# Group 0 of chunks 3 to 6 multiplied by blocks too, with one maximum instruction per head and the lower words behind the scaling

## The chip, the cores and the metric

The kernel runs on one core of a Trainium2 chip, in one launch. The time is device microseconds of the whole program. A core has a matrix engine (TensorE, PE in the profile, whose weight loads are listed as PEld), a vector engine (VectorE, DVE), a scalar engine (ScalarE, ACT), a general engine (GpSimd, POOL) and a queue that issues most DMAs (SyncE, SP). Each engine takes its instructions in the order in which the program lists them.

## The reference

All data is float32 (the inputs arrive as 64-bit floats and are scaled and split on the chip). Eight batches of eight heads attend over 576 positions of 64 values; scores that lie more than tau under the largest of their row are dropped. The heads are put side by side into rows of 512, and these 4608 rows go through a gated feed-forward block:

```python
scores = scale * np.matmul(q, k.transpose(0, 1, 3, 2))
thresh = np.max(scores, axis=-1, keepdims=True) - tau
scores = np.where(scores >= thresh, scores, -1000000000.0)
scores = scores - np.max(scores, axis=-1, keepdims=True)
attn = np.exp(scores)
attn = attn / (np.sum(attn, axis=-1, keepdims=True) + 1e-09)
x = np.matmul(attn, v)                 # (8, 8, 576, 64), then rows (4608, 512)
g = x @ w_gate                         # (512, 1536)
val = x @ w_val
out = (g / (1.0 + np.exp(-g))) * val @ w_out
```

## The kernel before

**Stages.** The work of the eight batches is interleaved. While the attention of batch b is computed, the feed-forward block of batch b - 1 ("chunk" c = b - 1) runs between its pieces. In the head (0 to about 126 us) the first batch's attention runs alone with a start of the feed-forward products, and the weights are split and joined from their 64-bit words: ScalarE takes the upper words (line 360) and the lower words (361), GpSimd clamps and adds (353, 397), VectorE shifts and joins (380, 387). From 126 to 1126 us come the main slots, 84 of them, and from there to 1334 us a tail with the products of the last batches.

**Main slots.** A pair of heads is done in three slots, so a chunk has twelve, kk = 0 to 11, of some 12 us each. A slot starts with the scores of two heads (`slot_scores`, 32 matmuls of 64x32 weights, line 2108) into two score tiles of two PSUM banks each (`ps_s`, a pool of two). Each head has three tiles u = 0, 1, 2 of 288 scores a partition. `slot_rest` then gives out jobs: VectorE finds the maximum of each tile (2129, 2131), the maxima of two partition groups are exchanged and joined (`largest` on VectorE, lines 2137 and 2138, or `others` on ScalarE, 2143, with 2147 on VectorE; the table MAX_BY_ACT says in which slots ScalarE does it), ScalarE computes a threshold (2150) and six exponentials (2154), VectorE six masks with their sums (2156), ScalarE exchanges the sums (2165), VectorE adds and inverts them (2171, 2172), ScalarE and GpSimd scale (2184, 2181; the table POOLED says how many tiles GpSimd takes), and VectorE transposes (2186). The next slot's scores write the same two tiles and wait for all six masks. In each slot with kk = 1, 4, 7, 10 the attention product of the pair before (`attend`, 2208) stands ahead of the scores.

**Gate and value products.** `gates_and_values(c)` goes through six groups g of 256 hidden columns. Each group takes seven products p1 to p7 instead of eight (a block scheme of Strassen's kind over two token halves and two halves of the model dimension), each of four matmuls of 128x128 weights with 256 moving columns, into three PSUM banks named pa, pb and pe. The banks come from four that are handed round (`take`). A copy of pa into pb by ScalarE starts the second accumulation. p5 and p3 go into pe, and ScalarE copies between them.

**Nested groups.** In chunks from DEEP = 2 on, some groups apply the scheme once more inside p5 and p3 (`NestedGroup`): seven matmuls of 128x128 weights and 128 moving columns into two banks in place of four of 256 columns. The inputs are quarters of the token sums that `deepen_x` makes on VectorE in slot kk = 1, from sums that GpSimd makes after the attention product of the same slot (`token_sums`). ScalarE copies both banks out (`Seven.fill`, 1320 and 1322), and four additions fold the seven results into a square (`Seven.fold`), on VectorE or GpSimd as the table FOLDS says. WITH_BLOCKS names the nested groups: 1, 2, 3 (in chunk 2 only 2 and 3). After a group's gate comes a hyperbolic tangent on ScalarE (1245), a multiplication on VectorE (1246) that frees the bank, and one on GpSimd.

**Output products.** `Deep` multiplies by the output weights in eight steps, in slots 9, 10, 11 and in slots 0 and 1 of the next chunk. Its last step, p3, stands in slot 1 between the scores and group 0's p1; its two banks are copied out by ScalarE (1839, 1840).

**Order.** Steps are generators. The table GV says how many steps of products follow the scores in slot kk: 3, 6, 4 in slots 1, 2, 3. Jobs of the other engines are ordered by a planner (`Plan`) when the program is built: each has a fixed planned length, dependences and a rank (0 first). The planner holds a clock per engine and puts the job next that could start first, rank before readiness; before each product it puts in the jobs that start by then. So the order of VectorE, ScalarE, GpSimd and the DMA queue is fixed when the program is built, and the chip adds only waits. Helpers record for many places: 968 is every GpSimd addition (`pool_tt`), 975 every VectorE one (`dve_tt`), 1187 every flat product (`Group.mul`), 1382 every nested one.

Of the kernel before, what the change touches and what calls it, by code (L numbers as in the profile page):

```python
# [157 lines left out]
def kernel(  # L158
# [12 lines left out]
    P = 128  # L171
# [27 lines left out]
    qkp = ctx.enter_context(tc.tile_pool(name="qkp", bufs=2))  # L199
    stp = ctx.enter_context(tc.tile_pool(name="stp", bufs=4))  # L200
    ps_s = ctx.enter_context(tc.tile_pool(name="ps_s", bufs=2, space=bass.MemoryType.PSUM))
    hbm = ctx.enter_context(tc.tile_pool(name="hbm", bufs=1, space=bass.MemoryType.DRAM))
# [151 lines left out]

    def split_weights():
        if fetched:
            dst, place = fetched.popleft()
            lo = los[0].rearrange("p (m n) -> p m n", m=dst.shape[1])
            los.rotate(1)
            nc.scalar.activation(dst, words(place, dst, 1).bitcast(F32), AF.Abs, scale=2.0 ** -96)  # L360
            nc.scalar.activation(lo, words(place, dst, 0), AF.Identity, bias=minus2, scale=-2.0 ** -51)
            unclamped.append(dst)
            if early_slots[0]:
                clamp_split()
            split.append((dst, place, lo))

    def clamp_split():
# [117 lines left out]
    def statistics(*names):  # L485
        return [stp.tile([P, 2 * NU3, 2] if x == "mx" else [P, 2 * NU3], F32, name=x) for x in names]

# [324 lines left out]
    for n, seg in enumerate(segs[:2 * NP]):  # L812
# [3 lines left out]
        for x, t in enumerate(seg["tiles"]):  # L816
# [39 lines left out]
            if n >= NP:  # L856
                split_weights()
                fetch_weights(2)
            steps(n, x, "flipped")
            next(go)  # L860
            steps(n, x, "masked")
            double = t == NT and NP <= n < NP + 3
# [447 lines left out]
    class Seven(Buf):  # L1310
# [6 lines left out]
        def fill(self, banks_, m, rank):  # L1317
            t, old = self.place, self.jobs
            self.jobs = []
            return [job("ACT", 0.46, lambda: nc.scalar.activation(t[:, 4 * P:CW], banks_[1].ap()[:, 0:3 * P], AF.Copy, scale=0.5),  # L1320
                        m, *old, rank=rank),
                    job("ACT", 0.57, lambda: nc.scalar.activation(t[:, 0:4 * P], banks_[0].ap(), AF.Copy, scale=0.5), m, *old, rank=rank)]  # L1322

# [28 lines left out]
    def deepen_x(c, *deps):  # L1352

        ts = *(x_main[:, n * 2 * P:(n + 1) * 2 * P] for n in range(3)), tmp.rearrange("p a f n -> p (a f n)")[:, 4 * HW:4 * HW + 2 * P]
        deps = *deps, *s_bufs[0].jobs
        t1, t2, t4, t3 = (x.rearrange("p (o q) -> p o q", o=2) for x in ts)
        x = xall[:, 3 * XW:3 * XW + 3 * HW].rearrange("p (o k n) -> p o k n", o=3, k=2)[:, 0:3:2]
        b11, b12, b21, b22 = (x[:, :, k_, n * P:(n + 1) * P] for k_ in range(2) for n in range(2))
        deps = *ready_x[c][1], *ready_x[c][4], *deps
        rank = 1  # L1360
        j = job("DVE", 0.36, dve_tt(t1, b12, b11, ALU.subtract), *deps, rank=rank)
        j = job("DVE", 0.36, dve_tt(t2, b22, t1, ALU.subtract), j, rank=rank)
        j = job("DVE", 0.36, dve_tt(t4, b21, t2, ALU.subtract), j, rank=rank)
# [728 lines left out]
    def slot_scores(seg, t):  # L2092
# [20 lines left out]
    def slot_rest(seg, t, pss, mark, pooled, max_by_act, rank):  # L2113
# [7 lines left out]
        at_of = lambda h, u: seg["p"] + (2 * (NU3 * t + u) + h) * SH  # L2121
        scs = {(h, u): pss[h][:, u, 0:SH] if u < 2 else pss[h][:, :, SH:SH + SQ] for h, u in tiles}
        flat = {x: pall[:, at_of(*x):at_of(*x) + SH] for x in tiles}
        ps = {x: y if x[1] < 2 else y.rearrange("p (a n) -> p a n", a=2) for x, y in flat.items()}
        n_of = lambda h, u: NU3 * h + u
        rs = []
        for h, tile_ in enumerate(pss):
            n = n_of(h, 0)
            rs.append(job("DVE", 0.72, lambda n=n, tile_=tile_: nc.vector.tensor_reduce(  # L2129
                out=mx[:, n:n + 2, 0], in_=tile_[:, :, 0:SH], axis=AX.X, op=ALU.max, negate=True), mark, rank=0))  # L2130
            rs.append(job("DVE", 0.42, lambda n=n, tile_=tile_: nc.vector.tensor_reduce(  # L2131
                out=mx[:, n + 2:n + 3, 0], in_=tile_[:, :, SH:SH + SQ], axis=AX.XY, op=ALU.max, negate=True), mark, rank=0))

        def largest():
            for g in range(NG):
                o = g ^ 1
                nc.vector.tensor_reduce(out=mx[g * G:(g + 1) * G, 0:m, 1], in_=mx[o * G:(o + 1) * G, 0:m, 0:1], axis=AX.X, op=ALU.max)
            nc.vector.tensor_reduce(out=nm[:, 0:m], in_=mx[:, 0:m, :], axis=AX.X, op=ALU.min)

        def others():  # L2140
            for g in range(NG):
                o = g ^ 1
                nc.scalar.copy(mx[g * G:(g + 1) * G, 0:m, 1], mx[o * G:(o + 1) * G, 0:m, 0])

        if max_by_act:
            oj = job("ACT", 0.78, others, *rs, rank=0)
            nj = job("DVE", 0.18, lambda: nc.vector.tensor_reduce(out=nm[:, 0:m], in_=mx[:, 0:m, :], axis=AX.X, op=ALU.min), oj, rank=0)
        else:
            nj = job("DVE", 0.82, largest, *rs, rank=0)
# [127 lines left out]
    def gates_and_values(c):  # L2277
# [490 lines left out]
```

## Time and profile before

| | us |
|---|---|
| median of 3 runs | 1332.65 (1332.35 to 1334.19) |
| profiled execution | 1336.15 |
| its span | 1334.4 |
| TensorE busy | 1323.6 (99%) |
| its weight loads busy | 1121.6 (84%) |
| VectorE busy | 1092.5 (82%) |
| GpSimd busy | 944.4 (71%) |
| ScalarE busy | 898.3 (67%) |
| scores start in slot 3 of chunks 3, 4, 5, 6 | 575.42, 719.40, 863.37, 1007.58 |

The profile is of one execution; a median is of several. The granted clock of TensorE is 1.00 over the whole span. A line of the timeline has the start in us from the span's start, the length, engine, line, operation, output and inputs, shapes and count; in brackets is the idle time before it and what ended it. Each float32 matmul leaves two records of TensorE, so a flat product shows as x8 and a nested one as 14 records in several lines. A list of waits has the waiting engine, tile and line, then what it waited for, the total, how many times, and the longest.

### The profile page before, as it was taken

The numbers are of one execution on the slowest core, as the hardware profiler recorded it, in microseconds if no ns is written. First come the engines' busy times: TensorE is split into PE (matmuls) and PEld (weight loads), VectorE is DVE, ScalarE is ACT, GpSimd is POOL, SyncE is SP. The second block draws the span as 40 slices with busy tenths as digits, with TensorE's granted clock in tenths as the row PEclk, the third lists the DMA queues.
The fourth block names the chain that finished last, engine by engine and source line by source line (L and its number), as shares of the span: only waits on it lengthen the run. The fifth ranks groups of instructions, "written<-read, shape, count | busy, mean of one in ns | idle before, by whom it ended". The sixth has DMA issues, their size and how long they took to land.

```text
span 1334.4 us, 41739 instructions
## 1 busy us (share of the span) xinstructions
PE 1323.6 (99%) x16294; PEld 1121.6 (84%) x16294; DVE 1092.5 (82%) x2900; ACT 898.3 (67%) x2343; POOL 944.4 (71%) x1130
## 2 busy tenths in 40 slices
PE   9999999999999999999999999999999999999998
PEld 7777777777888888888888888888888889999998
DVE  7889888888887787888888887888788888767987
ACT  6898876676756777787777777777778774444300
POOL 2688587565695969857895779677985798866720
PEclk9999999999999999999999999999999999999999
DMA  8863324456647653656365736655375627465341
GB/s 175 211 191 99 79 61 132 128 147 178 173 152 227 168 167 102 197 165 221 75 201 171 234 101 186 190 158 162 106 214 146 218 74 226 148 210 187 97 171 40
DMA packets 230884, 209.81 MB, mean 157 GB/s; under 512 B 167968, under 2 KB 185376, under 8 KB 223008
## 3 DMA queue, kind: packets, MB, share of 16 engines
q1 hardware_dynamic: 226768, 206.22, 52.5%
q8 instruction: 129, 2.11, 0.7%
q10 hardware_dynamic: 3920, 0.92, 0.3%
q14 instruction: 67, 0.55, 0.1%
HBM read 169.08 MB, written 38.01 MB: 155 GB/s over the span
## 4 chain that ended last, share of the span: by engine, by line
PE 93%; ACT 3%; DMA 1%; POOL 1%; DVE 1%; SPq 1%; issue 0%; ACTq 0%; DVEq 0%
PE pb L1187 14%; PE px L1817 12%; PE sc L2108 10%; PE pa L1187 10%; PE xa L2208 9%; PE pe L1187 6%; PE po L1495 6%; PE sc L2598 5%; PE py L1817 4%; PE pe L1382 3%; PE pb L2598 2%; PE pa L2598 2%; PE pg L1420 2%; PE pv L1420 2%; PE py L1826 2%; PE sc L502 1%
## 5 line engine op out<-in xcount | busy, mean ns | idle before, releaser
L2156 DVE SCALAR_TENSOR_TENSOR pall<-sc,th,pall 128x288 f32<-128x288 f32 x504 | 244.2, 514 | 39.5 <-ACT pall L2154 20.1
L2154 ACT ACTIVATE pall<-sc,nm 128x288 f32<-128x288 f32 x504 | 232.7, 497 | 35.3 <-DVE pall L2156 35.1
L1187 PE MATMUL pb<-xall,big 128*128 128x256 f32 x864 | 205.9, 381 | 0.0
L2186 DVE STREAM_TRANSPOSE pall<-pall 128x576 f32<-128x576 f32 x252 | 188.4, 764 | 19.2 <-ACT pall L2184 9.4
L968 POOL TENSOR_TENSOR big<-big 128x128 f32<-128x128 f32 (+3 forms) x226 | 167.2, 748 | 43.5 <-ACT big L1322 21.7
L2184 ACT ACTIVATE pall<-pall,ri 128x288 f32<-128x288 f32 x380 | 175.8, 527 | 28.2 <-DVE ri L2172 27.1
L1187 PEld LDWEIGHTS pb<-xall,big 128*128 128x128 f32 x864 | 161.0, 190 | 24.1 <-issue 2.2
L968 POOL TENSOR_TENSOR hall<-hall,tmp 128x512 f32<-128x512 f32 x80 | 102.1, 1278 | 88.0 <-DVE hall L1246 65.0
L2129 DVE TENSOR_REDUCE mx<-sc 128x2 f32<-128x576 f32 x168 | 125.6, 747 | 45.7 <-PE sc L2108 45.6
L2108 PE MATMUL sc<-kT,qT 64*32 64x288 f32 (+1 forms) x5376 | 144.5, 345 | 0.8 <-DVE pall L2156 0.8
L1187 PE MATMUL pa<-xall,big 128*128 128x256 f32 x576 | 137.6, 382 | 0.0
L2108 PEld LDWEIGHTS sc<-kT,qT 64*32 64x32 f32 x5376 | 95.2, 106 | 49.1 <-issue 8.3
L2208 PE MATMUL xa<-pall,vall 64*32 64x288 f32 x4032 | 128.7, 404 | 0.0
L1187 PEld LDWEIGHTS pa<-xall,big 128*128 128x128 f32 x576 | 107.9, 190 | 17.3 <-issue 2.2
L2208 PEld LDWEIGHTS xa<-pall,vall 64*32 64x32 f32 x4032 | 73.9, 107 | 47.0 <-issue 4.0
L2181 POOL TENSOR_SCALAR pall<-pall,ri 128x288 f32<-128x288 f32 x124 | 63.5, 524 | 49.7 <-DVE ri L2172 47.7
L2165 ACT COPY sums<-sums 32x6 f32<-32x6 f32 x336 | 66.6, 198 | 31.4 <-DVE pall L2156 26.3
L1187 PE MATMUL pe<-xall,big 128*128 128x256 f32 x352 | 83.9, 381 | 0.0
L2131 DVE TENSOR_REDUCE mx<-sc 128x1 f32<-128x288 f32 x168 | 75.0, 446 | 0.0
L1187 PEld LDWEIGHTS pe<-xall,big 128*128 128x128 f32 x352 | 66.3, 190 | 10.3 <-ACT xlast L2220 0.7
L968 POOL TENSOR_TENSOR hall<-hall 128x384 f32<-128x384 f32 (+2 forms) x69 | 70.5, 1034 | 0.8
L968 POOL TENSOR_TENSOR big<-hall 128x384 f32<-128x384 f32 (+2 forms) x69 | 65.7, 973 | 4.2 <-PE pa L1187 4.1
(400 smaller groups left out, 3065.4 us busy)
## 6 DMA issues: line engine op xcount, KB each, us to landing
big<-sums_hbm SPq DMA_DIRECT2D x30, 1280.0 KB, 7.5
big<-sums_hbm SPq DMA_DIRECT2D x30, 1024.0 KB, 8.1
vall<-in_v_dram SPq DMA_DIRECT2D x112, 144.0 KB, 4.1
big<-sums_hbm SPq DMA_DIRECT2D x54, 256.0 KB, 3.5
sums_hbm<-big SPq DMA_DIRECT2D x36, 256.0 KB, 3.6
out_dram<-big SPq DMA_DIRECT2D x32, 256.0 KB, 2.9
qT<-in_q_dram SPq DMA_DIRECT2D x112, 72.0 KB, 4.2
kT<-in_k_dram SPq DMA_DIRECT2D x112, 72.0 KB, 2.9
```

The lines of the kernel that those rows point to most:

```text
L968: nc.gpsimd.tensor_tensor(out=out, in0=a, in1=b, op=op)
L1187: nc.tensor.matmul(ps[:, i], w[:, k_, i * P:(i + 1) * P], x[:, k_, :], start=first and i == k_ == 0, stop=True, skip_group_check=True)
L1495: nc.tensor.matmul(ps, h(f), w[:, f, :], start=(f == 0), stop=(f == NF2 - 1))
L1817: nc.tensor.matmul(ps, a[:, f, :], ws[n][:, f, :], start=bank_ not in begun, stop=True, skip_group_check=True)
L2108: nc.tensor.matmul(pss[h][(slice(g * G, (g + 1) * G), *part)], qT[hs, col:col + G], kT[hs, c * SH + keys[0]:c * SH + keys[1]], start=True, ...
L2129: rs.append(job("DVE", 0.72, lambda n=n, tile_=tile_: nc.vector.tensor_reduce(out=mx[:, n:n + 2, 0], in_=tile_[:, :, 0:SH], axis=AX.X, op= ...
L2154: ej = job("ACT", 0.42, lambda x=x, n=n: nc.scalar.activation(ps[x], scs[x], AF.Exp, bias=nm[:, n:n + 1]), ej, masks.get((h, u - 1)), rank=0)
L2156: masks[x] = job("DVE", 0.45, lambda x=x, n=n: nc.vector.scalar_tensor_tensor(out=ps[x], in0=scs[x], scalar=th[:, n:n + 1], in1=ps[x], op0 ...
L2184: scaled.append(job("ACT", 0.46, lambda x=x, n=n: nc.scalar.activation(x, x, AF.Copy, scale=ri[:, n:n + 1]), rj, rank=rank))
L2186: seg["turned"].append(job("DVE", 0.72, lambda both=both: nc.vector.transpose(out=both, in_=both), *scaled, rank=rank))
L2208: nc.tensor.matmul(holds[a].ap()[x * G:(x + 1) * G, 0:SH].rearrange("d (i q) -> d i q", q=G), vr[rs, h, j, ds], p[rs, h, :, j, :], start=( ...
L2598: nc.tensor.matmul(both.ap(b_)[:, at_ * P:(at_ + 1) * P], ws[x], xd[x], start=b_ not in begun, stop=True, skip_group_check=True)
```

## The change

1. `WITH_BLOCKS` takes group 0 in: in chunks 3 to 6 groups 0 to 3 are nested, in chunk 2 still 2 and 3. In group 0 the steps stay in the order p1, p5, p2, p6, p3, p7.
2. The scores of a head are laid out so that the 864 scores of a partition are two runs of 432, one in each bank: tile 0 at the start of the first bank, tile 2 at the end of the second, tile 1 half at the end of the first and half at the start of the second. One VectorE instruction then finds the six maxima of 144 scores. What is exchanged has twelve columns instead of six, and the last joining takes four values for each tile. These maxima have a pool of their own with two buffers.
3. In the head, in the first step of the four later segments (`x == 0`), the activation of the lower words is put behind the exponentials' scaling.
4. `Seven.fill` copies the larger bank first. `deepen_x` has rank 0. The tables FOLDS, GV, POOLED and MAX_BY_ACT have other values: slot 2 has five steps and slot 3 five, slots 1, 3 and 9 exchange their maxima on VectorE, and the folds of the first nested product are on VectorE except in group 3, those of the second on GpSimd.

```diff
+    mxp = ctx.enter_context(tc.tile_pool(name="mxp", bufs=2))
...
+    late_lows = deque()
-    def split_weights():
+    def split_weights(late=False):
...
-            nc.scalar.activation(lo, words(place, dst, 0), AF.Identity, bias=minus2, scale=-2.0 ** -51)
+            late_lows.append((lo, place, dst))
+            if not late:
+                lower_words()
...
+    def lower_words():
+        while late_lows:
+            lo, place, dst = late_lows.popleft()
+            nc.scalar.activation(lo, words(place, dst, 0), AF.Identity, bias=minus2, scale=-2.0 ** -51)
...
-        return [stp.tile([P, 2 * NU3, 2] if x == "mx" else [P, 2 * NU3], F32, name=x) for x in names]
+        return [mxp.tile([P, 2, 4 * NU3], F32, name=x) if x == "mx" else stp.tile([P, 2 * NU3], F32, name=x) for x in names]
...
-                split_weights()
+                split_weights(x == 0)
                 fetch_weights(2)
             steps(n, x, "flipped")
             next(go)
+            lower_words()
...
         def fill(self, banks_, m, rank):
+            first = [job("ACT", 0.57, lambda: nc.scalar.activation(t[:, 0:4 * P], banks_[0].ap(), AF.Copy, scale=0.5), m, *old, rank=rank)]
             return [job("ACT", 0.46, lambda: nc.scalar.activation(t[:, 4 * P:CW], banks_[1].ap()[:, 0:3 * P], AF.Copy, scale=0.5),
-                        m, *old, rank=rank),
-                    job("ACT", 0.57, lambda: nc.scalar.activation(t[:, 0:4 * P], banks_[0].ap(), AF.Copy, scale=0.5), m, *old, rank=rank)]
+                        m, *old, rank=rank), *first]
...
-        rank = 1
+        rank = 0
...
-    FOLDS = ((0, 1, 2, 4, 5), (0, 2, 3, 5))
-    WITH_BLOCKS = (1, 2, 3)
+    FOLDS = ((3, 5), (0, 1, 2, 3, 5))
+    WITH_BLOCKS = (0, 1, 2, 3)
...
-            for u, part, keys in ((0, (0, slice(0, SH)), (0, SH)), (1, (1, slice(0, SH)), (0, SH)),
-                                  (2, (0, slice(SH, SH + SQ)), (0, SQ)), (2, (1, slice(SH, SH + SQ)), (SQ, SH))):
+            for u, part, keys in ((0, (0, slice(0, SH)), (0, SH)), (2, (1, slice(SQ, SQ + SH)), (0, SH)),
+                                  (1, (0, slice(SH, SH + SQ)), (0, SQ)), (1, (1, slice(0, SQ)), (SQ, SH))):
...
-            rs.append(job("DVE", 0.72, lambda n=n, tile_=tile_: nc.vector.tensor_reduce(
-                out=mx[:, n:n + 2, 0], in_=tile_[:, :, 0:SH], axis=AX.X, op=ALU.max, negate=True), mark, rank=0))
-            rs.append(job("DVE", 0.42, lambda n=n, tile_=tile_: nc.vector.tensor_reduce(
-                out=mx[:, n + 2:n + 3, 0], in_=tile_[:, :, SH:SH + SQ], axis=AX.XY, op=ALU.max, negate=True), mark, rank=0))
+            rs.append(job("DVE", 1.03, lambda h=h, tile_=tile_: nc.vector.tensor_reduce(
+                out=mx[:, 0, h * m:(h + 1) * m].rearrange("p (b c) -> p b c", c=NU3),
+                in_=tile_[:, :, 0:SH + SQ].rearrange("p b (c n) -> p b c n", n=SQ), axis=AX.X, op=ALU.max, negate=True), mark, rank=0))
...
-            deep = c >= DEEP and g in WITH_BLOCKS[c == DEEP:]
+            deep = c >= DEEP and g in ((2, 3) if c == DEEP else WITH_BLOCKS)
...
-            for fn in (new.p5, new.p2, new.p6, new.p3, new.p7) if not deep else (new.p2, new.p5, new.p6, new.p3, new.p7):
+            for fn in (new.p5, new.p2, new.p6, new.p3, new.p7) if not deep or g in (0,) else (new.p2, new.p5, new.p6, new.p3, new.p7):
...
-    GV = {1: 3, 2: 6, 3: 4, 4: 6, 5: 7, 6: 3, 7: 5, 8: 7, 9: 0}
+    GV = {1: 3, 2: 5, 3: 5, 4: 6, 5: 7, 6: 3, 7: 5, 8: 7, 9: 0}
...
-    POOLED = {NS: 2, 0: 3, 1: 1, 2: 1, 3: 3, 4: 3, 5: 2, 6: 1, 7: 2, 8: 1}
-    MAX_BY_ACT = (0, 1, 3, 4, 5, 6, 8, 9)
+    POOLED = {12: 2, 0: 2, 1: 3, 2: 1, 3: 3, 4: 1, 5: 3, 6: 1, 7: 1, 8: 1}
+    MAX_BY_ACT = (0, 4, 5, 6, 8)
```

More of the change, by code (lines that the diff above doesn't have):

```diff
@@ L2121, in slot_rest @@
         at_of = lambda h, u: seg["p"] + (2 * (NU3 * t + u) + h) * SH
-        scs = {(h, u): pss[h][:, u, 0:SH] if u < 2 else pss[h][:, :, SH:SH + SQ] for h, u in tiles}
+        step = 512 - SH
+        parted = [x.rearrange("p b n -> p (b n)")[:, SH:SH + 2 * step].rearrange("p (a n) -> p a n", a=2)[:, :, 0:SQ] for x in pss]
+        scs = {(h, u): parted[h] if u == 1 else pss[h][:, u // 2, u // 2 * SQ:u // 2 * SQ + SH] for h, u in tiles}
         flat = {x: pall[:, at_of(*x):at_of(*x) + SH] for x in tiles}
-        ps = {x: y if x[1] < 2 else y.rearrange("p (a n) -> p a n", a=2) for x, y in flat.items()}
+        ps = {x: y if x[1] != 1 else y.rearrange("p (a n) -> p a n", a=2) for x, y in flat.items()}
         n_of = lambda h, u: NU3 * h + u
@@ L2127, in slot_rest @@
         for h, tile_ in enumerate(pss):
-            n = n_of(h, 0)
-            rs.append(job("DVE", 0.72, lambda n=n, tile_=tile_: nc.vector.tensor_reduce(
-                out=mx[:, n:n + 2, 0], in_=tile_[:, :, 0:SH], axis=AX.X, op=ALU.max, negate=True), mark, rank=0))
-            rs.append(job("DVE", 0.42, lambda n=n, tile_=tile_: nc.vector.tensor_reduce(
-                out=mx[:, n + 2:n + 3, 0], in_=tile_[:, :, SH:SH + SQ], axis=AX.XY, op=ALU.max, negate=True), mark, rank=0))
+            rs.append(job("DVE", 1.03, lambda h=h, tile_=tile_: nc.vector.tensor_reduce(
+                out=mx[:, 0, h * m:(h + 1) * m].rearrange("p (b c) -> p b c", c=NU3),
+                in_=tile_[:, :, 0:SH + SQ].rearrange("p b (c n) -> p b c n", n=SQ), axis=AX.X, op=ALU.max, negate=True), mark, rank=0))
+        parts_of = mx.rearrange("p o (n a) -> p n o a", a=2)
         def largest():
@@ L2136, in largest @@
                 o = g ^ 1
-                nc.vector.tensor_reduce(out=mx[g * G:(g + 1) * G, 0:m, 1], in_=mx[o * G:(o + 1) * G, 0:m, 0:1], axis=AX.X, op=ALU.max)
-            nc.vector.tensor_reduce(out=nm[:, 0:m], in_=mx[:, 0:m, :], axis=AX.X, op=ALU.min)
+                nc.vector.tensor_reduce(out=mx[g * G:(g + 1) * G, 1, 0:2 * m], in_=mx[o * G:(o + 1) * G, 0, 0:2 * m].unsqueeze(2), axis=AX.X, op=ALU.max)
+            nc.vector.tensor_reduce(out=nm[:, 0:m], in_=parts_of, axis=AX.XY, op=ALU.min)
         def others():
@@ L2142, in others @@
                 o = g ^ 1
-                nc.scalar.copy(mx[g * G:(g + 1) * G, 0:m, 1], mx[o * G:(o + 1) * G, 0:m, 0])
+                nc.scalar.copy(mx[g * G:(g + 1) * G, 1], mx[o * G:(o + 1) * G, 0])
         if max_by_act:
             oj = job("ACT", 0.78, others, *rs, rank=0)
-            nj = job("DVE", 0.18, lambda: nc.vector.tensor_reduce(out=nm[:, 0:m], in_=mx[:, 0:m, :], axis=AX.X, op=ALU.min), oj, rank=0)
+            nj = job("DVE", 0.19, lambda: nc.vector.tensor_reduce(out=nm[:, 0:m], in_=parts_of, axis=AX.XY, op=ALU.min), oj, rank=0)
         else:
```

## The prediction, made before the changed kernel ran

> **What bounds the kernel now.** I read the page first, then TensorE's waits, then the timeline of all engines around one stretch, and last the busy time of the same stretch in four chunks. The page says that TensorE works all the time:
>
> ```profile
> span 1334.4 us, 41739 instructions
> PE 1323.6 (99%) x16294; PEld 1121.6 (84%) x16294; DVE 1092.5 (82%) x2900; ACT 898.3 (67%) x2343; POOL 944.4 (71%) x1130
> ```
>
> Of the 10.8 us in which it is idle, its list of waits explains under 7, nearly all before 150 us; in the main slots there is one wait in all:
>
> ```profile
> PE tp L573 <- ACT pall L539: 0.8, 2, 0.4
> PE sc L2108 <- DVE pall L2156: 0.8, 1, 0.8
> ```
>
> So this kernel can gain only what leaves TensorE, and it loses each microsecond that TensorE is made to wait. The profiled execution took 1336.15 us (span 1334.4, 1.75 around it); the median of the runs shown is 1332.65, so 3.5 lower. I work out a difference to the profiled execution and put it onto the median. 0.2% (2.7 us) is about what a measurement can tell from no change.
>
> **Products in group 0: TensorE's gain.** The timeline of TensorE in chunk 3 (start, length, line, count) has both forms of a product; a nested one ends where the next line starts:
>
> ```profile
> 568.42 1.89 PE L1187 MATMUL pb<-xall,big 128*128 128x256 f32 x8
> 570.15 1.89 PE L1187 MATMUL pa<-xall,big 128*128 128x256 f32 x8
> ...
> 580.46 0.61 PE L1382 MATMUL pe<-xall,big 128*128 128x128 f32 x4
> ...
> 582.02 1.89 PE L1187 MATMUL pb<-xall,big 128*128 128x256 f32 x8
> ```
>
> A flat product takes 570.15 - 568.42 = 1.73 us, a nested one 582.02 - 580.46 = 1.56. Chunks 3 to 6 get two each: 8 x 0.17 = 1.36 us less. It is not the eighth that seven products for eight promise (8 x 0.22 = 1.73): 14 records in 1.56 are 0.111 us each, where the flat ones pass 0.216.
> [...]
>
> **What the products wait for.** In group 0 the first nested product comes right behind the first flat one (557.94 to 559.67 in chunk 3), and it needs more than the flat one did. (a) Two banks: the second is one that the outputs' last product leaves at 557.94, and whose two copies in ACT ended at 559.17 here, 0.5 before the product starts. (b) The quarters of the token sums, four VectorE operations, of which the last ended at 561.34 here. Their rank goes from 1 to 0 and the order of instructions puts them between the first masks; walked through with the rows' lengths they start at 556.9 and end at 559.9, and the fourth is first read 0.67 after the product's start, at 560.3. Price of both between 0 and 4 x 0.4; I take 0, since 0.4 is left over.
>
> **VectorE in slots 1 and 2.** Here the cover is gone. Slot 3's scores may not start before slot 2's last mask, since both pairs of score banks are held until then. The table GV moves one step (a flat product, 1.73) from slot 2 to slot 3, and two nested products take 0.34 less, so TensorE comes to slot 3's scores 2.07 earlier: 575.42 - 2.07 = 573.35. Before, the last mask ended there:
>
> ```profile
> 573.10 0.52 DVE L2156 SCALAR_TENSOR_TENSOR pall<-sc,th,pall 128x288 f32<-128x288 f32 x1
> 573.54 0.08 DVE L2156 DVE_READ_ACCUMULATOR pall<-sc,th,pall 128x1 f32 x1
> ```
>
> at 573.62, already 0.3 too late; and VectorE had no room in the 20.2 us from slot 1's first maximum to that point, in any of the four chunks (length, then busy time of TensorE, its loads, VectorE, ...):
>
> ```profile
> 553.20:573.40 20.20, 20.20 (x172) 17.71 (x171) 19.19 (x55) 14.45 (x37) 12.52 (x19) 1.00 0.78 215
> 697.20:717.40 20.20, 20.20 (x170) 17.71 (x171) 19.22 (x55) 14.42 (x37) 12.53 (x20) 1.00 0.77 212
> 841.20:861.40 20.20, 20.20 (x170) 17.71 (x171) 19.28 (x55) 14.41 (x37) 12.53 (x19) 1.00 0.79 215
> 985.20:1005.40 20.20, 20.20 (x182) 17.63 (x170) 19.08 (x55) 14.57 (x38) 12.41 (x19) 1.00 0.77 216
> ```
>
> The change adds and removes VectorE work ahead of that mask, by these rows:
>
> ```profile
> 565.03 0.72 DVE L2129 TENSOR_REDUCE mx<-sc 128x2 f32<-128x576 f32 x1
> 565.68 0.45 DVE L2131 TENSOR_REDUCE mx<-sc 128x1 f32<-128x288 f32 x1
> 566.04 0.75 DVE L2129 TENSOR_REDUCE mx<-sc 128x2 f32<-128x576 f32 x1
> ...
> 567.19 0.64 DVE L2137 TENSOR_REDUCE mx<-mx 32x6 f32<-32x6 f32 x4
> ...
> 583.32 0.89 DVE L975 TENSOR_TENSOR big<-big 128x256 f32<-128x256 f32 x2 [0.29 <-ACT big L1322]
> ```
>
> - Slot 1 leaves MAX_BY_ACT: the four small maxima go to VectorE, +0.64.
> - The fold of group 0's first nested product: +1.55 to +1.88 (group 2's fold on VectorE took 0.80 for its first two operations, 0.29 and 0.79 for the others, the last beside POOL; undisturbed 3 x 0.42 + 0.29). I take 1.7.
> - The maxima: a pair passes in 0.65 + 0.36 = 1.01 (starts 565.03, 565.68, 566.04); 288 elements more cost about 0.30, so one instruction over 864 passes in 0.36 + 2 x 0.30 = 0.96. Four times 0.05 to 0.07: -0.25.
> - The multiplication at the end of the first half (0.60) moves behind the masks; the addition before it (0.61) stays ahead of them, and so do five transposes, as before.
>
> The sum is 0.64 + 1.7 - 0.25 - 0.60 = +1.5. Work up to the mask was 19.2 + 0.2, so 20.9, and from 553.29 without any idle time it ends at 574.2. ACT adds no more: group 0's copies of the second product (0.48 + 0.60, waiting for TensorE's end at 568.1) stand in its queue ahead of slot 2's exponentials, so that these start at 569.7 instead of 568.3, while VectorE reaches the first mask at 570.6 behind its transposes. Slot 3's scores then start at about 574.2, **0.8 late**. Between: 0 (if half of the fold and the small maxima fell into the 1.0 us idle and ran undisturbed) and 1.4 (if VectorE is idle as long as before). I take 0.8 four times: +3.2. TensorE does not make it up, and at the next product the copy to the second bank, which now queues behind this group's activations until about 575.8, is just in time.
> [...]
>
> **Other parts.**
> - The maxima elsewhere free about 0.1 us a slot of VectorE, where TensorE does not wait for it. Only at 146 us do scores wait for masks (0.8): -0.2, between 0 and -0.3.
> - Lower words behind the scaling: in two of the four steps the flips wait for a scaling that stands behind a lower-words activation, which itself waits for POOL:
>
> ```profile
> 96.27 1.02 ACT L361 ACTIVATE extra<-wo,minus 128x768 f32<-128x768 uint32 x1 [0.56 <-POOL big L397]
> 97.19 0.77 ACT L539 ACTIVATE pall<-pall,ri 128x576 f32<-128x576 f32 x1
> ```
>
> That wait (2 x 0.4) goes; next in line are the scores that started at 101.44 when VectorE's mask had ended at 101.38, behind weight joins that nothing here moves. So 0, at best -0.8.
> - Copies of a pair, larger bank first; the twelve-column maxima; two buffers for them, needed again two slots (24 us) later: 0 from rows in which TensorE waits for none of it.
> - POOLED, FOLDS, MAX_BY_ACT in other slots: the smallest distance from last mask to next scores is 0.3 us (before slot 8), and the order shows less VectorE work ahead of that mask (the addition now follows it). 0, at worst 4 x 0.3.
> - DMAs: none is added. The loads that slot 3 holds back hang on the last four steps, the same products as before, and SP passes them in the same order.
>
> **Sum:** -1.36 - 0.2 + 3.2 = +1.6 us, 1334.3 us.
>
> **Rivals.** (1) The cover holds: VectorE absorbs its new work and slot 3's scores wait at most 0.3 each. For it speaks that 1.0 us was idle; against it that the mask was late already. Then -1.4 to 0, around 1331.7. Chance 0.25. (2) The wait is larger, over 1.2 each, or the quarters or the second bank's copy come late as well (0.4 each): +3.3 to +5.4, around 1337.0. Chance 0.15. (3) Faster by over 0.2%: no wait at all, the head's 0.8 and the 0.8 at 146 us gone too: 1332.65 - 1.36 - 1.6 = 1329.7. It needs all of VectorE's lateness to vanish. Chance 0.05.
>
> **Numbers.** The forecast has 0.55, with a wait of 0.5 to 1.3 in each chunk: 1333.1 to 1336.3. Faster 0.05 is rival 3. Slower means over 1335.3: all of rival 2 and the upper quarter of the forecast, 0.15 + 0.14 = 0.29. The rest, 0.66, lies within 0.2%. The range goes from rival 1's middle, less its small gains, to rival 2's middle: 1330.9 to 1337.0.
>
> **What would show it.** 112 more records of 128x128 nested products and 64 fewer of 128x256 into the same banks; those pass in 1.56. Four waits of scores for masks at about 573, 717, 861 and 1005 us, 0.5 to 1.3 each, VectorE without idle time for some 20 us ahead of each. No wait at the first nested product of group 0, and no 0.4 at the flips near 98 and 117 us. The prediction is wrong if TensorE goes through slot 3 without a wait, or waits at another place.

## The result, and the profile after

The changed kernel takes 1338.1 us (median of 6 runs, 1336.88 to 1340.1), the kernel before 1332.62 beside it: a ratio of 1.0041 (1.0031 to 1.0051), so 5.5 us slower. Predicted were 1334.3, at most 1337.0.

TensorE has less to do and waits more. The page of the changed kernel, its two busiest lines:

```profile
span 1336.0 us, 41741 instructions
PE 1321.5 (99%) x16342; PEld 1121.4 (84%) x16342; DVE 1106.4 (83%) x2808; ACT 892.6 (67%) x2300; POOL 952.4 (71%) x1141
```

TensorE's list of waits (total, times, longest) has the scores behind the masks five times where before had them once, and a new wait of an attention product:

```profile
PE sc L2119 <- DVE pall L2168: 3.9, 5, 1.1
PE xa L2220 <- DVE hall L1257: 0.7, 1, 0.7
```

Four of the five are slot 3's scores of chunks 3 to 6 (1.14, 1.14, 0.63, 0.64 us of idle time). Here is chunk 3 in the timeline: TensorE's first nested product of group 0 and the scores, then VectorE's last masks with an addition between them, GpSimd, and ScalarE. The addition (L986 in VectorE's lines) finishes the first half of group 0's gate and is called g1 below; g2 is the like addition of the second half on GpSimd (L979, 569.70). L1256 is the tanh, L1205 the copy that opens the second bank of the next group:

```profile
557.10 0.61 PE L1393 MATMUL pe<-xall,big 128*128 128x128 f32 x4
...
558.66 1.89 PE L1198 MATMUL pa<-xall,big 128*128 128x256 f32 x8
...
572.00 2.14 PE L2119 MATMUL sc<-kT,qT 64*32 64x288 f32 x64 [1.14 <-DVE pall L2168]
574.08 1.99 PE L1198 MATMUL pa<-xall,big 128*128 128x256 f32 x8
```

```profile
569.63 0.51 DVE L2168 SCALAR_TENSOR_TENSOR pall<-sc,th,pall 128x288 f32<-128x288 f32 x1
570.07 0.08 DVE L2168 DVE_READ_ACCUMULATOR pall<-sc,th,pall 128x1 f32 x1
570.07 1.45 DVE L986 TENSOR_TENSOR tmp<-tmp,big 128x512 f32<-128x512 f32 x1
571.44 0.51 DVE L2168 SCALAR_TENSOR_TENSOR pall<-sc,th,pall 128x288 f32<-128x288 f32 x1
571.87 0.08 DVE L2168 DVE_READ_ACCUMULATOR pall<-sc,th,pall 128x1 f32 x1
571.87 0.51 DVE L2168 SCALAR_TENSOR_TENSOR pall<-sc,th,pall 128x288 f32<-128x288 f32 x1
...
566.97 2.76 POOL L979 TENSOR_TENSOR big<-big 128x256 f32<-128x256 f32 x4 [3.15 <-ACT big L1331]
569.70 1.26 POOL L979 TENSOR_TENSOR tmp<-tmp,big 128x512 f32<-128x512 f32 x1
...
571.55 1.15 ACT L1256 ACTIVATE vall<-tmp 128x512 f32<-128x512 f32 x2 [0.86 <-DVE tmp L986]
572.72 0.83 ACT L2177 COPY sums<-sums 32x6 f32<-32x6 f32 x4
573.46 0.57 ACT L1205 COPY pb<-pa 128x512 f32<-128x512 f32 x1
```

The nested product passes in 558.66 - 557.10 = 1.56 us without a wait. The scores begin when the mask ahead of the last (571.44) is done, wait inside for the last one too, and take 2.08 instead of 1.65 us. So each of the four costs more than its idle time. The copy into the second bank ends at 574.03, just ahead of the product that needs it (574.08). The measure I use below is the time from slot 2's scores to slot 4's: 26.49 us in chunks 3 and 4 and 25.99 in chunks 5 and 6, where before takes 25.02; by the work alone it should be 24.85 (one nested product, 0.17 less). That is 1.64, 1.64, 1.14 and 1.14 too much, 5.6 us in all.

The profile of before that the prediction used had a slow start; a second profile of the same kernel (below) has a span of 1331.5. Against that one the changed kernel's trace loses 4.5 us: 4.9 between slots 2 and 4, 0.8 at the attention product in chunk 6 and 0.8 between 124 and 157 us; it gains 0.6 between slots 1 and 2 and 1.4 in the rest, nearly all behind 1060 us.

### The profile page after: what moved, and what is told of

Its sections match the earlier page's. It is cut to its first block, busy times and chain, and to the rows that moved or that the text cites. A ratio compares the mean times of both kernels' runs of the same rounds, so it can differ in the third digit from the quotient of the medians.

```text
span 1336.0 us, 41741 instructions
## 1 busy us (share of the span) xinstructions
PE 1321.5 (99%) x16342; PEld 1121.4 (84%) x16342; DVE 1106.4 (83%) x2808; ACT 892.6 (67%) x2300; POOL 952.4 (71%) x1141
## 4 chain that ended last, share of the span: by engine, by line
PE 87%; DVE 7%; ACT 3%; issue 1%; DMA 1%; POOL 1%; SPq 0%; DVEq 0%; ACTq 0%
PE pb L1198 12%; PE px L1828 10%; PE sc L2119 10%; PE xa L2220 9%; PE pa L1198 8%; PE po L1506 6%; PE sc L2610 5%; PE pe L1198 5%; PE py L1828 4%; PE pe L1393 3%; PE pb L2610 2%; PE pa L2610 2%; PE pg L1431 2%; PE pv L1431 2%; PE py L1837 2%; DVE pall L2168 1%
## 5 line engine op out<-in xcount | busy, mean ns | idle before, releaser
L979 POOL TENSOR_TENSOR big<-big 128x128 f32<-128x128 f32 (+3 forms) x242 | 178.0, 745 | 54.1 <-ACT big L1331 32.3
L2141 DVE TENSOR_REDUCE mx<-sc 128x6 f32<-128x864 f32 x168 | 168.4, 1043 | 40.7 <-PE sc L2119 40.7
L2196 ACT ACTIVATE pall<-pall,ri 128x288 f32<-128x288 f32 x385 | 178.9, 529 | 21.5 <-DVE ri L2184 20.4
L979 POOL TENSOR_TENSOR hall<-hall,tmp 128x512 f32<-128x512 f32 x80 | 102.1, 1279 | 68.6 <-DVE hall L1257 41.7
L979 POOL TENSOR_TENSOR hall<-hall 128x384 f32<-128x384 f32 (+2 forms) x69 | 70.4, 1035 | 0.8
L979 POOL TENSOR_TENSOR big<-hall 128x384 f32<-128x384 f32 (+2 forms) x69 | 66.6, 991 | 6.1 <-PE pa L1198 6.0
L1198 PE MATMUL pe<-xall,big 128*128 128x256 f32 x288 | 68.9, 382 | 0.0
L979 POOL TENSOR_TENSOR tmp<-tmp 128x256 f32<-128x256 f32 (+3 forms) x52 | 49.3, 957 | 22.3 <-ACT tmp L1279 9.8
L2162 ACT ACTIVATE th<-nm,cut 128x6 f32<-128x6 f32 x84 | 25.1, 299 | 59.3 <-DVE nm L2150 48.0
```

Of the source, the lines that this page charges most:

```text
L979: nc.gpsimd.tensor_tensor(out=out, in0=a, in1=b, op=op)
L1198: nc.tensor.matmul(ps[:, i], w[:, k_, i * P:(i + 1) * P], x[:, k_, :], start=first and i == k_ == 0, stop=True, skip_group_check=True)
L2141: rs.append(job("DVE", 1.03, lambda h=h, tile_=tile_: nc.vector.tensor_reduce(out=mx[:, 0, h * m:(h + 1) * m].rearrange("p (b c) -> p b c" ...
L2196: scaled.append(job("ACT", 0.46, lambda x=x, n=n: nc.scalar.activation(x, x, AF.Copy, scale=ri[:, n:n + 1]), rj, rank=rank))
```

## The experiments

Line numbers of an experiment can be some higher than those of the changed kernel. All times are medians, with the kernel before run beside them (1332.45 to 1332.79). The last column is the time from slot 2's scores to slot 4's in chunks 3 and 5.

| kernel | us | ratio to before | slots 2 to 4 |
|---|---|---|---|
| before | 1332.6 | 1 | 25.02 / 25.01 |
| changed | 1338.1 | 1.0041 (1.0031 to 1.0051) | 26.49 / 25.99 |
| e2 steps 6, 4 | 1347.2 | 1.0116 (1.0096 to 1.0135) | 27.75 / 27.80 |
| e3 first fold to GpSimd by the table | 1336.8 | 1.0034 (1.0020 to 1.0047) | 26.44 / 25.90 |
| e4 before, group 0 nested | 1351.7 | 1.0146 (1.0133 to 1.0160) | 29.75 / 27.74 |
| e5 g2 behind g1, order free | 1365.9 | 1.0246 (1.0232 to 1.0259) | 34.41 / 33.43 |
| e6 slot 1 maxima by the table | 1365.3 | 1.0240 (1.0226 to 1.0254) | 32.84 / 32.17 |
| e7 group 0 flat | 1335.4 | 1.0019 (1.0010 to 1.0028) | 25.88 / 25.02 |
| e8 before, one maximum | 1333.8 | 1.0007 (0.9999 to 1.0016) | 25.02 / 25.02 |
| e9 small maxima, order kept | 1337.2 | 1.0029 (1.0018 to 1.0041) | 26.48 / 25.95 |
| e10 g1 behind masks | 1339.2 | 1.0046 (1.0033 to 1.0059) | 26.81 / 26.30 |
| e11 fold on GpSimd, order kept | 1335.9 | 1.0022 (1.0013 to 1.0031) | 25.92 / 25.90 |
| e12 before, lower words | 1332.3 | 0.9994 (0.9985 to 1.0003) | 25.02 / 25.02 |
| e13 e11, g2 behind g1 | 1336.6 | 1.0030 (1.0019 to 1.0042) | 26.05 / 26.06 |
| e14 e13, second tanh behind copy | 1338.2 | 1.0040 (1.0026 to 1.0054) | 25.82 / 25.83 |
| e15 group 0 flat, steps 6, 4 | 1334.2 | 1.0009 (1.0001 to 1.0018) | 25.02 / 25.02 |

### Where the loss sits

**e1**, the kernel before, unchanged.

> The kernel before, unchanged, for a second profile. In the shown profile of before the first 20 us lost 2.3 us against the changed kernel, and its execution was 3.5 us over the median. If that was one slow start, a second profile has its scores of chunk 0, slot 0 near 123.8 us (126.17 in the first) and a span near 1331; if the change itself gained there, it stays at 126.2 and 1334.

Its span is 1331.5, its time 1333.3, and slot 0's scores start at 123.81. It had been one slow start: TensorE's second block of matmuls, in the first profile and in this one,

```profile
7.64 2.30 PE L502 MATMUL first<-pall,qT 64*128 64x288 f32 x8 [1.46 <-DVE cap L741]
```

```profile
6.74 1.25 PE L502 MATMUL first<-pall,qT 64*128 64x288 f32 x8 [1.24 <-DVE cap L741]
```

ran at nearly half the rate. What slowed it the records do not show (both list a clock of 1.00 there). Nor does this profile have the wait of 0.8 at 146 us: the scores there follow at once. That wait is in one of the two executions and not in the other.

**e2**, the moved step put back:

```diff
-    GV = {1: 3, 2: 5, 3: 5, 4: 6, ...
+    GV = {1: 3, 2: 6, 3: 4, 4: 6, ...
```

> The changed kernel with the step that moved to slot 3 put back to slot 2 (GV 6 and 4). TensorE then comes to slot 3's scores 1.73 us later. Theory A (VectorE's backlog in slots 1 and 2 sets the start of slot 3's scores): the four waits, with the parts inside the scores 1.64, 1.64, 1.15 and 1.15 us, go, and the kernel takes about 1338.1 - 5.6 = 1332.5. Theory B (the nested products of group 0 themselves, or the other parts, cost the time): waits move to another place and the time stays within 1 us of 1338.

1347.2, 9 us slower than the changed kernel; the profiled execution took 1343.9 (the end of this document says what parts the two). Slot 3's scores wait no more, but the product that now stands ahead of them does:

```profile
PE pa L1198 <- ACT pb L1205: 11.2, 4, 3.2
```

The end of the chain of work that e2's product waited for (start, length, engine, line):

```profile
569.82 1.40 DVE tmp L986
571.24 1.15 ACT vall L1256 x2
572.42 0.20 ACT sums L2177
...
573.24 0.49 ACT pb L1205
573.73 0.04 issue
573.77 1.99 PE pa L1198 x8
```

This is the addition g1, the two tanh, ScalarE's exchange of sums, and the copy into the second bank, that of group 1's first product. Ahead of g1 stand VectorE's masks; GpSimd's fold, which g1 needs too, had ended 0.3 us before it. In a flat group 0 the addition reads the products' bank itself; nested, the product is first copied out by ScalarE and folded by GpSimd. So GV's 5 and 5, which puts slot 3's scores ahead of this product, hides the longer chain. Neither theory of the expectation had it; I call it theory F.

**e3**, the fold by the table: `FOLDS = ((0, 3, 5), ...`.

> The changed kernel with one edit: the fold of group 0's first nested product is on GpSimd, as it is for most groups in before. VectorE loses 1.4 to 2.1 us of work ahead of slot 2's last mask. Theory A: the waits of slot 3's scores shrink by that, to 0 in chunks 5 and 6 and at most 0.3 in chunks 3 and 4: about 1333. Rival C (the addition of VectorE beside GpSimd, 1.45 instead of 0.6 us, is what makes the mask late): the addition still runs beside GpSimd, and with GpSimd busier by 2.8 us the waits stay above 0.5: above 1335. Theory B: 1338.

1336.8. Slots 2 to 4 win 0.05 and 0.09 only; most of the gain is the attention product of chunk 6, which no longer waits. VectorE's order had changed as well: a transposition of qT stood behind the last mask (wait of 1.3 in chunk 3). The time is the one that rival C gave, though g1 took only 0.94 in chunks 3 and 4 (1.46 in 5 and 6). The sum of VectorE's work alone does not give the wait.

**e4**, before with group 0 nested and nothing else:

```diff
-    WITH_BLOCKS = (1, 2, 3)
+    WITH_BLOCKS = (0, 1, 2, 3)
```

(with the two conditions on g of the change that go with it).

> The kernel before with group 0 nested and nothing else: tables, maxima, fill order and lower words as before, both folds of group 0 on GpSimd, six steps in slot 2. Theory A: TensorE comes to slot 3's scores 0.34 earlier and VectorE has no more work ahead of them than before, so the gain of eight products (8 x 0.17 = 1.36) stays but for 4 x 0.3: 1331.3 to 1332.5, against 1332.6. Theory B (the nested products of group 0 cost time by their own needs: quarters of the token sums at rank 1, two banks): slower than 1333.5, with waits at the first nested product at 558, 702, 846 and 990 us.

1351.7. The chain of F again, and the quarters of the token sums, which have rank 1 here, come late:

```profile
PE pa L1187 <- ACT pb L1194: 11.2, 4, 3.0
PE pe L1382 <- DVE tmp L975: 3.5, 4, 0.9
```

So nested with before's rank and tables, group 0 costs 19 us; what the rank and each table are worth by themselves no run parts. Theory B's waits at the first nested product are there (3.5 us), but most of the loss is F's. Theory A fell in its simple form.

### Parts

**e5** adds `*((self.g1,) if self.g == 0 and self.c > DEEP else ())` to the dependences of g2; **e6** has `MAX_BY_ACT = (0, 1, 4, 5, 6, 8)`.

> The changed kernel, but in group 0 of chunks 3 to 6 GpSimd's addition to the second half (g2, beside VectorE's addition g1 until now) waits for g1. Theory C (the two additions slow each other: g1 took 1.45 us and g2 1.26): g1 takes 0.6 to 0.95, the waits of slot 3's scores fall by 0.5 to 0.85 each: 1338.1 - 2.0 to 3.4, so 1334.7 to 1336.1. Rival: g1 takes 1.4 by its own size, nothing changes, 1338. Work behind slot 3's scores is in another order in this kernel, which can add waits of its own there; the start of slot 3's scores is the measure.

> The changed kernel with slot 1 back in MAX_BY_ACT: ScalarE exchanges the maxima (0.8 us of its time) and VectorE loses the four small maxima, 0.67 us. Theory A: VectorE's backlog and so the waits of slot 3's scores fall by up to 0.67 in each of four chunks: 1335.4 to 1337. Rival E (the last masks wait for ScalarE's exponentials, not for VectorE's own work): the waits stay, 1338 or slower.

Both came out at 1365 to 1366 and tell little of what they were made for. The planner put other work first; in e5 slot 2's sums went behind slot 3's maxima (577.59 instead of 573.59), and with them the scaling and the transpositions for slot 4's attention product, which then started behind a gap of 4.5 us. e6 has that gap too, in all four chunks. g1 was not parted from g2 either: g2 started at 569.88 and g1 at 570.27, and g1 took 1.44 us. A dependence given to the planner orders the program's instructions, but it put no wait between these two on the chip. In e6 slot 3's scores did start 1.2 earlier. From here on I kept every queue's order and changed only what the program emits at a place. What a gap of 4.5 us does besides is told at the end.

**e7**, group 0 flat in the changed kernel: `WITH_BLOCKS = (1, 2, 3)`.

> The changed kernel with group 0 flat again, all other parts (one maximum instruction, lower words, tables) kept. Theory A: 1.36 us of TensorE come back, the fold (1.4 to 2.1 us of VectorE) and its wait go: 1338.1 - 5.6 + 1.4 = 1333.9, with 0.8 less if the attention product in chunk 6 no longer waits. Theory B (the other parts cost): 1338 to 1339.5.

1335.4: 2.7 less than the changed kernel, though it has eight more flat products. Slots 2 to 4 still lose 0.86 in chunks 3 and 4, since with five steps slot 3's scores come before qT is transposed (0.60 us of idle time). That is between theory A's 1333.9 and theory B's 1338.

**e8**, before with the score layout and one maximum instruction per head.

> The kernel before with the score layout and the one maximum instruction per head, nothing else. By the rows, 0.05 to 0.07 us of VectorE for each pair of instructions, which TensorE feels only at 146 us: 1332.2, between 1332.0 and 1332.6. Theory D (an order of VectorE that is off by a little anywhere makes scores wait): slower than 1334, with waits of scores for masks in slots where before has none.

1333.8, by the ratio 0.9 slower (interval -0.1 to +2.1): not the small gain that was expected, and no loss that this can tell for certain. Two of the new instructions take 2.02 us (at 550.72 in the changed kernel), the four old ones 2.16 (from 601.87 in before).

### With every queue in its order

**e9**: in slot 1 of chunks 3 to 6 ScalarE copies the maxima at the same place.

```diff
-            nj = job("DVE", 0.82, largest, *rs, rank=0)
+            nj = job("DVE", 0.82, by_act if swapped else largest, *rs, rank=0)
```

> The changed kernel with every queue in its order, but in slot 1 of chunks 3 to 6 the four small maxima (0.67 us) are taken by ScalarE at the same place of the program. Theory A (VectorE's backlog alone sets slot 3): slot 2's last mask and slot 3's scores come up to 0.67 earlier and TensorE keeps it: 1338.1 - 2.7 = 1335.4. Theory F (a chain sets the next product too: nested product p3, its copy on ScalarE, fold on GpSimd, addition g1, tanh, multiplication, copy into the second bank, product pa; it ends at 573.95 us in chunk 3, just before pa at 574.14): g1 comes at most 0.3 earlier since the fold ends at 569.70, so 4 x 0.3: about 1337.

1337.2, theory F's number, and slots 2 to 4 are unchanged (0.01 and 0.04 less). VectorE has 0.67 less to do and idles 0.87 for ScalarE instead, at the same place of its queue:

```profile
553.46 0.18 DVE L2159 TENSOR_REDUCE nm<-mx 128x6 f32<-128x24 f32 x1 [0.87 <-ACT mx L2155]
```

Of the 0.9 that the time fell, 0.8 are chunk 6's attention product, which does not wait here.

**e10**: g1, and the tanh that needs it, emitted behind slot 2's last mask.

```diff
-            g1 = job("DVE", 0.62, dve_tt(u.ap, u.ap, e.ap, ALU.add), j, self.u1, rank=0)
+            add = dve_tt(u.ap, u.ap, e.ap, ALU.add)
+            if self.late:
+                add_now, add = add, lambda: later.append(add_now)
+            g1 = job("DVE", 0.62, add, j, self.u1, rank=0)
...
+                if x == (1, NU3 - 1):
+                    put_late()
```

> The changed kernel with every queue in its order, but in group 0 of chunks 3 to 6 VectorE's addition g1 (1.45 us) stands behind slot 2's last two masks instead of ahead of them. Theory A: the last mask ends 1.4 us earlier, slot 3's scores start at 571.1 instead of 572.0 without a wait inside, and TensorE keeps it: 1338.1 - 5 = 1333. Theory F: the scores do start earlier, but g1, tanh, multiplication and the copy into the second bank come no earlier, and the product behind the scores waits for that copy instead (1.2 us and more): 1338, within 0.7.

1339.2, 0.5 above theory F's range and 6 above theory A's 1333. This run tells the theories apart. TensorE in chunk 3, and g1:

```profile
570.34 2.14 PE L2138 MATMUL sc<-kT,qT 64*32 64x288 f32 x64
573.89 1.99 PE L1199 MATMUL pa<-xall,big 128*128 128x256 f32 x8 [1.42 <-ACT pb L1206]
...
570.64 0.69 DVE L986 TENSOR_TENSOR tmp<-tmp,big 128x512 f32<-128x512 f32 x1
```

The scores start without idle time, 1.15 earlier against slot 2, and the next product waits 1.42 for the copy into the second bank. Theory A's 5 us are not there: the masks were one of two limits that ended within 0.1 us of each other (574.03 and 574.08 in the changed kernel). Apart from GpSimd the addition takes 0.69.

**e11**: the first fold runs on GpSimd at its place, VectorE's order kept (`tt = pool_tt` inside the fold for group 0).

> The changed kernel with VectorE's order kept, but group 0's first fold runs on GpSimd at the same place of the program (in the run with that fold given to GpSimd by the table, VectorE's order changed too and a transposition came to stand behind the last mask). VectorE loses 2.0 us in chunk 3, 1.5 in chunk 5, of which the maxima, which wait for slot 2's scores, can use 0.8. Theory A: waits of slot 3's scores fall by 0.8: 1338.1 - 3.2 = 1335. Theory F: the chain through GpSimd's second fold comes at most 0.3 earlier: about 1337.

1335.9, between the two theories: 0.57 and 0.09 less in slots 2 to 4, and chunk 6's 0.78. VectorE now waits for slot 2's scores (0.38 us, at 561.89), so nothing is left over from slot 1; still slot 3's scores wait:

```profile
571.06 2.14 PE L2121 MATMUL sc<-kT,qT 64*32 64x288 f32 x64 [0.56 <-DVE pall L2170]
...
569.04 1.52 DVE L986 TENSOR_TENSOR tmp<-tmp,big 128x512 f32<-128x512 f32 x1
...
568.75 1.27 POOL L979 TENSOR_TENSOR tmp<-tmp,big 128x512 f32<-128x512 f32 x1
```

Slot 2 by itself, from its scores to its last mask, is longer than the five steps that cover it.

**e12**, before with the lower words behind the scaling.

> The kernel before with the lower words behind the scaling, nothing else. The prediction's 0 (at best -0.8): two flips near 96 and 115 us lose a wait of 0.4 each, and the scores behind them wait instead. In six traces with the part the scores of chunk 0, slot 0 start at 123.1 to 123.7 us, in three without it (the slow start apart) at 123.8 to 124.1: I expect 0.1 to 0.7 earlier, so 1332.0 to 1332.6.

1332.3 against 1332.8, ratio 0.9994 (0.9985 to 1.0003). The waits of the flips at 96 and 114 us are gone, and the scores behind the first of them wait 0.40 for a mask instead.

### Both chains

**e13** is e11, with g2 held until g1 is done: GpSimd first reads one element that g1 wrote.

```diff
+                    y = self.added.ap[:, 0, 0:1]
+                    nc.gpsimd.tensor_tensor(out=one[:, 0:1], in0=y, in1=y, op=ALU.add)
                     add()
```

> As the run with group 0's first fold on GpSimd and the orders kept (1335.9), and GpSimd's addition g2 waits for g1 in chunks 3 to 6 (one element of g1's output is read first; no queue is reordered). g1 should then take 0.7 instead of 1.5 us and slot 2's last mask end 0.8 earlier, near 570.6 in chunk 3. Theory A (masks alone): 1335.9 - 4 x 0.8 = 1332.7. Theory F (the copy into the second bank sets the next product): g2 ends near 571.2, the second tanh, the exchange of sums and the copy stand behind it on ScalarE, the copy ends at 573.1 as before, and the product behind the scores waits instead: 1335.9 within 0.5.

1336.6, no faster than e11 and 4 above theory A's 1332.7. g1 takes 0.69, the scores start 0.64 earlier against slot 2, and the product behind them waits:

```profile
569.08 0.69 DVE L986 TENSOR_TENSOR tmp<-tmp,big 128x512 f32<-128x512 f32 x1
...
573.31 1.99 PE L1201 MATMUL pa<-xall,big 128*128 128x256 f32 x8 [0.92 <-ACT pb L1208]
```

**e14** is e13 with the second tanh emitted behind the copy on ScalarE.

> As the run before it, and on ScalarE the second tanh of group 0 stands behind the copy into the second bank instead of ahead of it. Theory F: masks end near 570.6 and the copy near 572.1, so that TensorE goes through slot 3's scores and the next product with 0.3 or less of waiting: 1335.9 - 4 x 0.75 = 1332.9, and down to 1331.7 if all of the 1.05 us a chunk that is left comes back. Theory A or B: no gain over the run before it. The second half's multiplication comes 0.8 later by this, with VectorE's next maxima behind it; if that shows, scores of slot 4 wait.

1338.2, and not theory F's 1332.9. Scores and the next product now go through without idle time in all four chunks, as expected, and yet slots 2 to 4 win only 0.1 over e11. The wait is now one product further on:

```profile
576.23 1.89 PE L1207 MATMUL pb<-xall,big 128*128 128x256 f32 x8
578.52 0.71 PE L1441 MATMUL pe<-xall,big 128*128 128x128 f32 x4 [0.39 <-ACT big L1377]
...
577.68 0.30 ACT L2219 ACTIVATE th<-nm,cut 128x6 f32<-128x6 f32 x1 [1.23 <-DVE nm L2207]
577.89 0.58 ACT L1377 ACTIVATE big<-pe 128x512 f32<-128x512 f32 x1
```

Group 1's second nested product needs the copy of its first, which stands on ScalarE behind a threshold, which waits for slot 3's maxima, which VectorE reaches later because the second multiplication came later. The rest of the slowdown against e11 lies elsewhere: one load from HBM lands 1.2 late in chunk 6, 0.25 in slot 4 of each chunk, and 0.6 at 146 us.

**e15**, group 0 flat and steps 6 and 4.

> The changed kernel with group 0 flat and six and four steps in slots 2 and 3 as before; what is left of the change is the maximum instruction, the lower words, the order of a pair's copies, the rank of the quarters and the tables of folds, scaling and maxima. If those cost nothing: before's 1332.6 less 0.3 to 0.5 for the lower words, 1332.2, and no wait at slot 3. If they cost: above 1333.5.

1334.2, with no wait at slot 3 and 25.02 in slots 2 to 4. So the parts beside group 0 and its steps cost 0.1 to 2.4 us over before, and group 0 with its steps the other 3.9 of the 5.5 (1338.1 - 1334.2). Which of those parts costs it no run shows.

## Why the prediction was wrong

**The products** were right: 1.56 instead of 1.73.

**What the products wait for** was right at 0: no idle time at 557.10. e4, with rank 1 and the old tables, waits 0.9 a chunk there.

**VectorE in slots 1 and 2** is the step that failed, by the size of one term. Place, sign and the near absence of idle time were right: from slot 1's first maximum to the end of slot 2's last mask (550.72 to 572.39 in chunk 3) VectorE is busy for 21.10 of 21.67 us. The length was not: the sum had 20.9, and the trace has 21.67 in chunks 3 and 4 and 21.2 in 5 and 6. So the 0.8 a chunk, 3.2 in all, became 1.64, 1.64, 1.14 and 1.14, 5.6 in all. (The idle times alone, 1.14 and 0.63, lie within the 0.5 to 1.3 that the prediction named; what the scores lose inside comes on top.) The mis-sized term is the addition ahead of the masks, "(0.61) stays ahead of them". In a flat group it reads PSUM, and the next instruction starts 0.61 later (569.31 behind 568.70 in before). In a nested group both inputs lie in SBUF, and it starts while GpSimd's addition runs: it is 1.45 us long, and the next mask starts 1.37 later, 0.76 more than the sum had. Where GpSimd does not run it is 0.69 long (e10 and e13). The trace of before had both lengths of this form, alone at 586.63 and beside GpSimd at 604.00:

```profile
586.63 0.68 DVE L975 TENSOR_TENSOR tmp<-tmp,big 128x512 f32<-128x512 f32 x1
...
604.00 1.20 DVE L975 TENSOR_TENSOR tmp<-tmp,big 128x512 f32<-128x512 f32 x1
```

and the prediction passed them by. The fold was nearly right (1.7; 2.0 in chunk 3, 1.5 in chunk 5). The small maxima, priced at 0.64 a chunk, were worth nothing in e9: ScalarE's exchange takes as long (VectorE idles 0.87 us for it, for 0.67 of work less). Nor does the sum hold term by term: with the fold taken off VectorE (e11) 0.57 and 0.09 us came back of its 2.0 and 1.5, since other limits stand right behind.
The traces show when the long form ends: GpSimd's addition ends at 570.96, g1 at 571.52, 0.56 later; in e3 570.69 and 571.24; in e11 570.02 and 570.56, so 0.54 to 0.56 each time, however long g1 was. What holds g1 up they do not show.

**"At the next product the copy ... is just in time"** was right (574.03 for 574.08), but the prediction put no price on it: it is a second limit, not slack. From slot 2's scores to this copy's end it is 13.54 us in chunk 3 of the changed kernel, 13.87 in e10, 12.97 in e11 and 13.11 in e13, and slots 2 to 4 take 26.49, 26.81, 25.92 and 26.05: the same differences within 0.01. So with the masks out of the way (e10, e13) this chain alone holds nearly all of the time; only in e14, with 11.83 and 25.82, does another limit hold. The missing chain is p3, ScalarE's copy, GpSimd's fold, g1, tanh, multiplication, exchange, bank copy; a flat group 0 lacks two of its members. It does not stand apart from VectorE's load: TensorE has done p3 at 565.7 in the changed kernel, but ScalarE's copy of it (566.32) stands behind slot 2's threshold (566.11), which waits for VectorE's maxima.

**146 us, -0.2**: the wait in the profile used was that of one execution; e1 has none, and the changed kernel's profile has 0.38. **Lower words, 0**: right within e12's interval. **Other slots, 0**: e15 has 0.1 to 2.4, and the addition of 1.76 us beside GpSimd at 1052.12 made chunk 6's attention product wait 0.72 (in e3, e9, e11 and e13 the same addition starts ahead of GpSimd's and takes 0.75 to 0.77, and the product does not wait); the bound of "4 x 0.3" held only slots' masks in view. **The maxima, -0.25**: two instructions fewer a slot saved 0.14 (2.02 us in the changed kernel, 2.16 in before), as the rows had it (two pairs at 0.05 to 0.07).

Of the 3.8 us that the forecast was too low, 2.4 are the waits ahead of and inside slot 3's scores (5.6 for 3.2), 0.7 the attention product; the rest lies in the other parts. Rival 2, a wait of over 1.2 each, is the nearest: true in chunks 3 and 4, just missed in 5 and 6 (1.14), and the whole, +5.5, lies just above its +3.3 to +5.4.

## What to carry to other kernels

Price an instruction by a row with the same operands and the same neighbours: an addition with both inputs in SBUF has two prices here, 0.69 alone and up to 1.76 beside GpSimd. Where something ends "just in time", write it down as the next limit, and price what removing the first one would leave; in slots 2 to 4 three limits (the masks, the copy into the second bank, a copy behind a threshold) stood within about a microsecond, and each run that took one away found the next. A product that is faster on TensorE but hands its result through two more engines needs that latency covered. Here, where TensorE is busy 99% of the time, the cover was a step moved behind slot 3's scores, and it was taken from the masks.

## What the runs showed of the hardware

TensorE's granted clock fell to 0.50 behind some gaps. In e5, e4 and e2, stretches with TensorE's busy time (first after the length) and the granted clock (third from the end):

```profile
583.20:587.70 4.50, 0.02 (x1) 0.02 (x1) 3.57 (x7) 4.14 (x11) 3.09 (x4) 0.92 0.00 0
590.00:591.00 1.00, 1.00 (x28) 1.00 (x20) 0.83 (x2) 0.04 (x1) 1.00 (x3) 0.50 0.06 16
593.00:594.00 1.00, 1.00 (x28) 1.00 (x20) 0.00 (x0) 0.00 (x0) 0.00 (x1) 0.59 0.00 0
594.00:595.00 1.00, 1.00 (x45) 1.00 (x36) 0.00 (x0) 0.00 (x0) 0.00 (x0) 1.00 0.00 0
```

```profile
576.00:578.00 2.00, 2.00 (x13) 1.08 (x18) 1.86 (x3) 0.95 (x3) 1.92 (x5) 0.50 0.11 45
```

```profile
1008.00:1026.00 18.00, 15.33 (x181) 12.36 (x187) 15.40 (x44) 13.01 (x31) 9.98 (x15) 1.00 0.43 155
```

Behind a gap of 4.50 us in e5 the clock was 0.50 from 587.00 to 593.83 (read in slices of 0.1 us), and the attention product took 7.70 us instead of 4.60. In e4 it fell behind gaps of 2.99, 2.98 and 2.62 us: from 575.32 to 578.73, from 725.50 to 728.92 and from 1022.46 to 1025.88. In e2's profile gaps of 2.6 to 3.2 left it at 1.00. In chunk 3 of e4 the half clock cost 1.64 us beside the gap of 2.99 (from the late product to the next nested one it is 5.21 us, in e2 3.57).

Each of e4's falls lasts 3.41 or 3.42 us, e5's 6.83. In e4's chunk 5 a gap of 2.62 us (871.17 to 873.79) left the clock at 1.00, while behind the gap of the same length in chunk 6 (1019.03 to 1021.65) it fell. So the same wait can cost half its length more (1.64 us beside 2.99 in chunk 3), or not; what decides it was not shown. e2's six executions part by the clock as well: 1343.9 and 1344.5 us at a mean granted clock of 1.000, 1346.3 at 0.998, 1348.2 at 0.996, 1351.5 and 1352.6 at 0.994. About 3 of the 9 us by which its median is slower than the changed kernel are therefore clock, not waits (an estimate: 1347.2 less the 1343.9 to 1344.5 at 1.000).
